# One fixed work list for another: the same 1368 tasks of a fused attention and MLP kernel, reordered

## The chip, the cores and the metric

The kernel runs on one core of a Trainium2 chip. The core's engines run their own instruction streams beside each other and meet only at semaphores: TensorE (PE, the matrix unit, with its weight loads shown as PEld), VectorE (DVE), ScalarE (ACT), GpSimd (POOL), and SyncE (SP), whose queue here issues nearly all DMA transfers. The metric is the device time of one execution in microseconds (us); the time given for a kernel is the median of its runs.

## The reference

A pre-norm block on 2048 tokens of width 640, in bfloat16, with two halves:

```
h  = x + attention(layernorm(x)) @ wo        # 32 heads of 20, four segments of 512 tokens
h2 = h + silu(layernorm(h) @ w1) @ w2        # 640 -> 1728 -> 640
```

Inside a segment the attention is causal softmax. From the second segment on, each head also reads a memory: with `phi(t) = t + 1 if t > 0 else exp(t)`, a matrix `M` and a vector `z` collect `phi(k)^T v` and the sum of `phi(k)` of all earlier segments, `a_mem = phi(q) M / (phi(q) z + 1e-6)`, and the output is `g * a_mem + (1 - g) * a_dot` with `g = sigmoid(beta)` of the head.

## The kernel before

The kernel is a graph of 1368 small tasks. Each is declared once (lines 550 to 1215) with the buffers that it reads and writes, its possible engines, and a function that emits its instructions. A list that is written out in the kernel, the string `ORDER`, fixes three things: the order of all tasks (each engine runs its own tasks in the order in which they stand in the list), the engine where a task has a choice (`/A` ACT, `/D` DVE, `/S` SP), and the buffer slots that a task opens (the numbers after the colon: PSUM banks, and slots of small rotating buffers). A tracker derives the semaphore waits from the reads and writes. There is no planner at run time: the list is the schedule.

The token dimension is cut into 16 blocks of 128 (`b`) and four segments of four blocks (`s`). The names in the list are these, in the order in which one segment's data passes through them:

- Loads: `x0` to `x12`, `w_wv`, `w_q`, `w_k`, `beta`, `w_wo`, `w_w1_0` to `w_w1_4`, `w_w2_0` to `w_w2_5` (lines 562 to 574). `beta` is a broadcast of 64 bytes to each of 128 partitions. `fillN` is N matmuls on zeros that have no use but to keep TensorE active (L599). `re_wq*`, `re_wk*` copy the raw weights into head groups (L677 on ACT, L679 on DVE); the raw weights land in the tile `sT`.
- Layer norm: `n1_st` (statistics, DVE, L706 and L709), `n1_rs` (POOL, L715 and L717), `n1_ap` (DVE, L723). For the first four blocks the transposition is done on TensorE, `n1_tp` (L732), and copied out by `n1_te` (ACT L741 or DVE L742); for all others by a DMA, `n1_tr` (L747).
- Projections: `v` (L774) and its evacuation `ve` (ACT L784, DVE L785); `pr` + segment + group + 0 for q or 1 for k (L808), its evacuation `qe` (ACT L816, DVE L817); `ex` (exponential, ACT L823) and `ph` (DVE L830, L833) make phi; `vt` are DMAs that build the head groups 5 to 7 (L844).
- Scores: `qk` (L880) computes a score set of four heads into four PSUM banks. The number after its colon is the first bank, so `:0` is banks 0 to 3 and `:4` is banks 4 to 7; two ACT exponentials `e...0` and `e...2` (L891) read two banks each into `PTA`, `PTB` or `PTE`; `mk` masks the diagonal on POOL (L903); `av` multiplies with v (L926). A tick is then finished by `oe` (ACT L939, DVE L941), `tn` (TensorE, L955 and L959), `nm` (DVE, L972 to L992) and `ad` (POOL, L1000). In segment 0 the score sets carry the suffixes `x`, `ya` and `yb` after the group; in the later ones `a`, `b`, `e` after `8 * s + g`.
- Memory of a segment: `kt` (DMA transposition), `mz` (L1048), `ma` (L1077), `mb` (POOL, L1084).
- Output projection and MLP: `ot` (DMA transposition), `wo` (L1109), `rs` (DVE, L1117), `n2_*` (the second layer norm, as above), `h1` (L1143, its narrow last slice L1138), `th` (tanh, ACT, L1152), `s` (DVE, L1158), `h2` in four parts (L1176), `o` (DVE, L1186), `out` (store).

Nearly all `qk` of a segment use the same four banks as the `qk` before them. Such a `qk` can start only when both exponentials of the set before have read those banks, and ACT can start on the new set only when the `qk` is done. Between the two sets ACT has work only if the list puts some other ACT task there.

Of the kernel before, what the change touches and what calls it, by code (L numbers as in the profile page):

```python
# [324 lines left out]
D = 640  # L325
# [45 lines left out]
n1_ap7:3 epsg1 oe4x/D:0 ve12/D kt02:0 n1_tr7 w_w1_2/S w_w2_0/S kt00:1 w_w1_3/S ex011:0 mk1yb mk5x mt0 qk6x0:4 av0y:2
e6x0:1 e6x2 tn4x:3 oe0y/D:0 av5x:0 tn3x:1 oe5x/A:1 qk7x0:4 e7x2:0 e7x0 nm4x:3 v10:2 nm3x:0 qk2ya0:4 ph041:2
n1_st10:2 ve10/D e2ya0:0 e2ya2 n1_rs11 mta2 mk7x n1_st9:3 n1_rs10 v13:0 mk6x tn0y:2 av7x:3 ve13/D nm0y:1 qk2yb0:4
oe7x/A:0 e2yb2:0 e2yb0 tn5x:3 tn7x:0 nm7x:2 av1y:1 av6x:2 qk3ya0:4 oe6x/D:1 nm5x:3 w_w1_4/S tn6x:2 nm6x:0 ot1:0
w_w2_5/S ot0 w_w2_4/S w_w2_1/S oe1y/A:0 e3ya0:1 e3ya2 ph011:1 pr101:1 mtb3 mz02:2 mk2yb av2y:3 qk3yb0:4 e3yb0:1
e3yb2 ma02/D:0 mz00:2 tn1y:0 oe2y/D:1 n1_ap11:1 qe101/D:0 pr100:3 qk4ya0:4 e4ya0:0 e4ya2 mk3yb ex031:2 nm1y:1
qe100/D wo1:0 av3y:3 qk4yb0:4 e4yb2:0 e4yb0 ma00/D:1 tn2y:2 ex101:1 rs1 wo0:0 oe3y/D:0 n2_st1:5 nm2y:2 kt04:0 tn3y:3
n2_rs1 nm3y:3 rs0 qk5ya0:4 pr140:2 n1_rs8 mk4yb pr121:3 e5ya0:1 e5ya2 qe140/A:0 qk5yb0:4 e5yb2:1 e5yb0 ex140:0
pr141:0 av4y:2 n2_ap1:0 n2_st0:4 n2_rs0 n2_ap0:2 kt01:1 n2_tr1:0 qk6ya0:4 qe141/D mk5yb pr120:1 ph031:0 oe4y/D:1
pr111:0 qe121/D:0 e6ya0:0 e6ya2 qk6yb0:4 qe120/D ex121:2 av5y:3 n2_tr0 h1_0_7_0:1 h1_0_0_0:2 e6yb2:0 e6yb0 qk7ya0:4  # L380
th0_7_0:0 ph101:2 qe111/D:0 oe5y/D:0 tn4y:0 s0_7_0:0 th0_0_0:1 h1_0_8_0:3 nm4y:0 s0_0_0 mz01:1 mz04:0 ma01/D:2
h1_0_3_0:2 e7ya2:1 e7ya0 th0_8_0:0 ma04/D:3 s0_8_0 th0_3_0:1 s0_3_0 tn5y:1 qk7yb0:4 e7yb2:1 mk6yb e7yb0 mk7yb mta0
av6y:0 mtb0 oe6y/A:1 h1_0_12_0:3 h1_0_1_0:2 qk8a0:4 th0_1_0:0 e8a2:0 e8a0 th0_12_0:1 s0_1_0 pr110:0 nm5y:1 qe110/D
h1_0_10_0:2 av7y:1 qk8e0:4 oe7y/D:0 th0_10_0:0 s0_12_0 pr130:0 s0_10_0 e8e2:0 e8e0 h1_0_5_0:2 h1_0_11_0:3 qk8b0:4
th0_5_0:1 n1_ap8:3 qe130/D:0 th0_11_0:0 w_w2_2/S kt03:1 tn7y:0 s0_5_0 nm7y:2 mz03:1 s0_11_0 h1_0_2_0:2 e8b2:0 e8b0
ma03/D:4 h1_0_6_0:0 th0_2_0:1 h1_0_13_0:1 th0_13_0:0 qk9a0:4 pr131:3 s0_2_0 s0_13_0 n1_ap10:0 h1_0_4_0:1 h1_0_9_0:2
qe131/D e9a2:1 e9a0 mk8a mk8e mm0 th0_6_0:1 th0_4_0:0 ex100:1 s0_6_0 mm4 mk8b mm6 qk9b0:4 vt19:0 th0_9_0:1 mm2 mm8
n1_rs9 mtb2 s0_4_0 w_w2_3/S vt16 vt10 vt18 e9b2:1 e9b0 av8:3 h2_0_0:0 h2_0_1 qk10a0:4 s0_9_0 ph100:0 ex141:1 ph121:1
e10a2:0 e10a0 h2_0_2 tn6y:2 h2_0_3 ph141:0 ex120:2 mk9a qk10b0:4 oe8/D:0 nm6y:3 o0 mzc0 mzc6 ph120:0 mzc2 h2_1_0:2
mk9b mm10 mzc4 e10b0:0 kt10:0 vt15 mm1 mzc1 mb00:0 e10b2 mk10a mzc5 mzc8 mm7 mzc7 mb03:0 mk10b ex111:1 n1_tr10:0  # L390
tn8:0 vt11 n1_tr8 nm8:0,0 h2_1_1 vt13 ot2 ot3 qk10e0:4 ph111:2 vt111 kt12:1 vt17 vt110 vt12 h2_1_2 av9:0 h2_1_3
ex110:2 ph110:0 oe9/D:1 e10e0:1 e10e2 qk11a0:4 mk10e mm3 mzc3 mb01:0 wo3:0 ad8:0 n1_ap9:2 o1 n1_tr9 vt14 e11a2:1
n1_tr11 e11a0 ex131:1 av10:2 mk11a mzc10 qk11b0:4 e11b0:1 e11b2 mk11b mb02:0 mm9 mzc9 rs3 oe10/D:0 tn9:0 wo2:2
qk12a0:4 nm9:1,1 v20:0 rs2 n2_st3:6 ex130:2 ph130:0 e12a2:0 e12a0 av11:2 qk13a0:4 n2_st2:7 mz12:3 ma12 ve20/A:0
# [851 lines left out]
```

## Time and profile before

| | us |
|---|---|
| median of 3 runs (305.32 to 306.07) | 305.46 |
| span of the profiled execution | 303.9 |
| TensorE busy / idle in the span | 290.1 / 13.8 |
| ScalarE (ACT) busy | 226.8 (75%) |
| VectorE (DVE) busy | 219.1 (72%) |
| GpSimd (POOL) busy | 143.9 (47%) |
| share of the chain that ended last: PE / ACT / DVE / DMA | 72% / 12% / 7% / 4% |

The span runs from the first to the last instruction of one profiled execution; the median of the runs lies 1.5 us above it. A busy time is the time in which an engine had an instruction running. For TensorE that is an upper bound of useful work, since the end of a matmul is modelled and a matmul in flight counts as busy while the next waits. TensorE's share is 95% over the whole span, but the other engines' shares are averages over stages with different limits: ACT has hardly anything to do in the last 55 us, which belong to the MLP of the last two segments, and is busy nearly all the time in some earlier stretches.

### The profile page before, as it was taken

The numbers are of one execution on the slowest core, as the hardware profiler recorded it, in microseconds if no ns is written. First come the engines' busy times: TensorE is split into PE (matmuls) and PEld (weight loads), VectorE is DVE, ScalarE is ACT, GpSimd is POOL, SyncE is SP. The second block draws the span as 40 slices with busy tenths as digits, with TensorE's granted clock in tenths as the row PEclk, the third lists the DMA queues.
The fourth block names the chain that finished last, engine by engine and source line by source line (L and its number), as shares of the span: only waits on it lengthen the run. The fifth ranks groups of instructions, "written<-read, shape, count | busy, mean of one in ns | idle before, by whom it ended". The sixth has DMA issues, their size and how long they took to land.

```text
span 303.9 us, 7238 instructions
## 1 busy us (share of the span) xinstructions
PE 290.1 (95%) x2876; PEld 165.8 (55%) x2900; DVE 219.1 (72%) x489; ACT 226.8 (75%) x322; POOL 143.9 (47%) x280
## 2 busy tenths in 40 slices
PE   8799889999999999999999999999999999999995
PEld 5434454466555455566644545566564466764573
DVE  5677997886788877877989886558767486835523
ACT  4599998999989889989789899968878941005310
POOL 4237673525677856535758328434873730300000
PEclk9999999999999999999999999999999999999999
DMA  6678487643153130056561500043250004332001
GB/s 194 216 211 240 79 202 179 130 106 90 38 110 61 41 41 2 4 102 64 132 170 22 67 17 19 2 77 62 36 108 2 0 2 88 80 88 72 0 24 65
DMA packets 48433, 24.64 MB, mean 81 GB/s; under 512 B 38864, under 2 KB 47312, under 8 KB 48400
## 3 DMA queue, kind: packets, MB, share of 16 engines
q1 hardware_dynamic: 47728, 23.09, 33.9%
q10 hardware_dynamic: 672, 1.10, 1.2%
q8 instruction: 23, 0.38, 0.5%
q14 instruction: 10, 0.08, 0.1%
HBM read 10.41 MB, written 2.62 MB: 43 GB/s over the span
## 4 chain that ended last, share of the span: by engine, by line
PE 72%; ACT 12%; DVE 7%; DMA 4%; issue 2%; POOL 1%; SPq 1%; DVEq 0%; ACTq 0%
PE ps_all L1176 18%; PE ps_all L1143 16%; PE ps_all L808 12%; PE ps_all L1109 7%; PE ps_all L880 6%; PE ps_all L926 5%; ACT PTA L891 4%; ACT PTB L891 3%; DMA sT<-in_A_wq_dram 3%; PE ps_all L774 2%; PE ps_all L955 2%; ACT PTE L891 2%; PE ps_all L959 1%; DMA oT<-otok 1%; PE ps_all L1048 1%
## 5 line engine op out<-in xcount | busy, mean ns | idle before, releaser
L891 ACT ACTIVATE PTA<-ps_all 128x1024 bf16<-128x1024 f32 x64 | 62.1, 1027 | 7.1 <-PE ps_all L880 6.5
L1176 PE MATMUL ps_all<-w_sb,sT 128*128 128x320 bf16 x448 | 65.2, 299 | 0.0
L891 ACT ACTIVATE PTB<-ps_all 128x1024 bf16<-128x1024 f32 (+1 forms) x64 | 58.9, 971 | 5.9 <-PE ps_all L880 5.6
L1143 PE MATMUL ps_all<-hT,w_sb 128*128 128x512 bf16 (+1 forms) x315 | 60.1, 335 | 0.9 <-issue 0.5
L1152 ACT ACTIVATE th<-ps_all 128x512 f32<-128x512 f32 (+2 forms) x70 | 34.0, 507 | 35.3 <-PE ps_all L1143 26.8
L1158 DVE SCALAR_TENSOR_TENSOR sT<-th,ps_all 128x512 bf16<-128x512 f32 (+2 forms) x70 | 38.0, 561 | 27.0 <-ACT th L1152 25.8
L903 POOL TENSOR_SCALAR_AFFINE_SELECT PTB<-PTB 128x512 bf16<-128x512 bf16 x64 | 41.3, 647 | 32.6 <-ACT PTB L891 30.3
L1176 PEld LDWEIGHTS ps_all<-w_sb,sT 128*128 128x128 bf16 x448 | 42.3, 98 | 19.3 <-issue 2.1
L1143 PEld LDWEIGHTS ps_all<-hT,w_sb 128*128 128x128 bf16 x325 | 30.3, 98 | 23.9 <-issue 1.3
L891 ACT ACTIVATE PTE<-ps_all 128x1024 bf16<-128x1024 f32 (+1 forms) x40 | 35.4, 943 | 2.2 <-PE ps_all L880 2.1
L903 POOL TENSOR_SCALAR_AFFINE_SELECT PTE<-PTE 128x512 bf16<-128x512 bf16 x40 | 26.0, 649 | 20.3 <-ACT PTE L891 18.8
L706 DVE BATCH_NORM_STATS2 stt<-x_tok 128x6 f32<-128x320 bf16 x64 | 27.9, 477 | 1.6 <-DMA x_tok<-in_A_x_dram 1.4
L808 PE MATMUL ps_all<-xT,wqr 128*128 128x512 bf16 x92 | 23.4, 380 | 1.9 <-ACT xT L741 1.1
L774 PE MATMUL ps_all<-wv_sb,xT 128*128 128x320 bf16 x160 | 24.3, 300 | 0.7 <-DMA xT<-xn_rot 0.4
L1109 PE MATMUL ps_all<-wo_sb,oT 128*128 128x320 bf16 x160 | 24.1, 299 | 0.8 <-DMA oT<-otok 0.5
L1000 POOL TENSOR_TENSOR otok<-on 128x320 bf16<-128x320 bf16 x24 | 19.0, 793 | 11.3 <-DVE on L992 11.3
L808 PE MATMUL ps_all<-xT,wkr 128*128 128x512 bf16 x94 | 23.4, 380 | 0.5 <-issue 0.3
L903 POOL TENSOR_SCALAR_AFFINE_SELECT PTA<-PTA 128x512 bf16<-128x512 bf16 x24 | 15.5, 647 | 16.5 <-ACT PTA L891 16.4
L1186 DVE SCALAR_TENSOR_TENSOR x_tok<-ps_all,x_tok 128x640 bf16<-128x640 f32 x16 | 13.0, 818 | 13.8 <-PE ps_all L1176 13.8
L880 PE MATMUL ps_all<-QK 20*128 20x256 bf16 (+3 forms) x360 | 20.5, 286 | 1.7 <-ACT PTB L891 0.7
L992 DVE TENSOR_TENSOR on<-ps_all,rd 128x640 bf16<-128x640 f32 x24 | 19.8, 825 | 0.8
L715 POOL TENSOR_TENSOR rst<-mvt,eps_c 128x1 f32<-128x1 f32 x32 | 7.0, 219 | 27.9 <-DVE mvt L709 24.9
(79 smaller groups left out, 412.6 us busy)
## 6 DMA issues: line engine op xcount, KB each, us to landing
out_dram<-x_tok SPq DMA_DIRECT2D x16, 160.0 KB, 1.9
w_sb<-in_B_w_dram SPq DMA_DIRECT2D x4, 432.0 KB, 6.0
w_sb<-in_B_w_dram SPq DMA_DIRECT2D x3, 480.0 KB, 4.3
x_tok<-in_A_x_dram SPq DMA_DIRECT2D x2, 640.0 KB, 4.4
QKV<-QK SPq DMA_DIRECT2D x16, 72.0 KB
wv_sb<-in_A_wv_dram SPq DMA_DIRECT2D x1, 800.0 KB, 5.6
sT<-in_A_wq_dram SPq DMA_DIRECT2D x1, 800.0 KB, 7.8
sT<-in_A_wk_dram SPq DMA_DIRECT2D x1, 800.0 KB, 9.6
```

The lines of the kernel that those rows point to most:

```text
L706: T.add(DV, lambda e, hh=hh: e.bn_stats(out=stt[:, s, 6 * hh:6 * hh + 6], in_=xb[:, 320 * hh:320 * hh + 320]), reads=R((xa, xsub)), writes ...
L774: fns.append(lambda e, c=c, hh=hh: e.matmul(bank(ps, hh)[:, 0:320], lhsT=xT[:, c, 128 * i:128 * i + 128], rhs=wv_sb[:, c, 320 * hh:320 * h ...
L808: fns = [lambda e, kc=kc: e.matmul(bank(ps)[:, lo:hi], lhsT=wt[:, kc, c, :], rhs=xT[:, kc, lo:hi], start=(kc == 0), stop=(kc == NC - 1)) f ...
L880: fns.append(lambda e, j=j, o=o, r=r, q0=q0, q1=q1, qa=qa, ka=ka: e.matmul(ps_all[:, o:o + q1 - q0], lhsT=ka[32 * r:32 * r + DH, 128 * j:1 ...
L891: T.add(AC, lambda e: e.activation(out=pt[:, pta.slot, q0:q0 + 2, 0:width], in_=sc3[:, b0:b0 + 2, 0:width], func=ACT.Exp, scale=SCALE), re ...
L903: fns.append(lambda e, v=v: e.affine_select(out=v, in_=v, pattern=[[0, 4], [1, 128]], compare_op=ALU.is_ge, fill=0.0, base=0, channel_mult ...
L992: T.add(DV, lambda e: e.tensor_tensor(out=on[:, ona.slot, :, :].rearrange("p b (x e) -> p b x e", e=DH), in0=v[:, :, :, 0:DH], in1=r2.unsq ...
L1109: fns.append(lambda e, c=c, hh=hh: e.matmul(bank(ps, hh)[:, 0:320], lhsT=oT[:, c, 128 * i:128 * i + 128], rhs=wo_sb[:, c, 320 * hh:320 * h ...
L1143: fns = [lambda e, c=c: e.matmul(bank(ps)[:, lo:hi], lhsT=w1_sb[:, c, 128 * f:128 * f + 128], rhs=hT[:, c, lo:hi], start=(c == 0), stop=(c ...
L1152: T.add(AC, lambda e: e.activation(out=th[:, tha.slot, lo:hi], in_=bank(ps)[:, lo:hi], func=ACT.Tanh, scale=0.5), reads=R((ps, [0])), writ ...
L1158: T.add(DV, lambda e: e.scalar_tensor_tensor(out=sT[:, f, lo:hi], in0=th[:, tha.slot, lo:hi], scalar=1.0, in1=bank(ps)[:, lo:hi], op0=ALU. ...
L1176: fns.append(lambda e, f=f, t0=t0, fr=fr, hh=hh: e.matmul(bank(ps, hh)[:, 0:320], lhsT=sT[:, f, t0:t0 + 128], rhs=w2_sb[:, fr, 320 * hh:32 ...
```

## The change

The string `ORDER` is replaced by another one, of the same 1368 tasks. It was annealed in a replay of the trace: order on each engine, engine of the evacuations, and slots. No task's function is touched, and every matmul, exponential and transfer is still there. What differs, beyond many swaps of neighbours:

- Start. `x1, x0, x2, x3` are loaded ahead of `w_wv`, `w_q`, `w_k`, and `beta` comes after `w_k` (before: `x0, x1, w_wv, x2, x3, beta, w_q, w_k`). The 31 `fill` matmuls of the start stand in one row (before: 21, then 6 and 4 between later transpositions). `v01` comes after all transpositions, and the `pr`/`qe` and `re_*` tasks of the first groups change order and engine.
- Queues. `x8` and `w_w1_0` move from ACT's DMA queue to SP's; the order of the MLP weights on SP is another one.
- Engines. 45 tasks change engine. In the projections of the last segment `qe310, qe311, qe321, qe340, qe341, ve31, ve33` go from ACT to DVE; `oe22, oe24` from DVE to ACT. In the middle of the list `ve23, qe211, qe230` go from DVE to ACT, `qe221, oe14` from ACT to DVE.
- TensorE's order is the same from the second score set on but for swaps over short distances, until the end of the last segment's attention. There `wo12, wo13, wo15, wo14` (before `wo14, wo12, wo15, wo13`) and the `h1_3` and `h2` groups of the last two segments take another order.

```diff
-zpad:0 x0:0 x1:1 w_wv:0 x2:2 x3:3 beta w_q:0 w_k halfc warm:0 iota vpad0 sel n1_st0:0 n1_st1:1 epsc mt3 vpad1 n1_rs0
-n1_rs1 epsg0 n1_ap0:0 fill21:0 n1_tp0:0 n1_te0/A:0 n1_ap1:1 fill6:2 n1_tp1:2 n1_te1/A v00:0 v01:2 n1_st2:2 n1_rs2
-n1_st3:3 n1_rs3 mt1 mt2 mta1 n1_ap2:2 n1_ap3:3 n1_tp2:4 n1_te2/D re_wq1/A:0 fill4:6 n1_tp3:6 n1_te3/A pr010:6
-re_wk1/D:0 re_wk0/D re_wk3/D x4/S:4,5,6,7 pr011:4 re_wk2/D re_wq4/D qe011/D:0 ve00/A:0 re_wk4/A qe010/A re_wq2/A
-lsc0 pr001:0 ve01/D lsc1 lsc2 re_wq0/A qe001/A:0 qk1x0:4 e1x2:0 pr000:1 qe000/D lsc3 pr021:0 e1x0 mk1x qk0x0:4
...
-kt20:0 ve32/D e22b2:1 e22b0 pr330:1 ex241:2 th1_8_0:0 qk23a0:4 e23a0:0 e23a2 pr310:2 qe310/A:0 qe330/D:0 pr301:3
-ex310:0 s1_8_0 tn19:0 qk22e0:4 ph221:2 qe301/D:0 pr300:2 pr311:3 e22e0:1 e22e2 qk23b0:4 ex240:1 qe311/A ph241:1
...
-th2_5_0:0 s2_5_0 th2_10_0:0 s2_12_0 h2_8_0:2 h2_11_0:4 h1_2_11_0:7 h2_8_1 h2_11_1 ad30 ot14:0 th2_11_0:1 wo14:0
-s2_10_0 s2_11_0 ot12 rs14 n2_st14:2 ot15 wo12:6 rs12 n2_st12:3 wo15:0 h2_11_2 h2_11_3 h2_8_2 rs15 n2_rs14 ot13
...
+iota:0 zpad warm:0 sel halfc x1:8 fill4:6 fill21:0 fill6:2 n1_st1:2 vpad1 mt3 x0:5 x2:0 n1_st0:0 x3:1 n1_st2:1 w_wv:0
+epsc mt0 n1_rs1 n1_rs0 n1_ap0:0 n1_ap1:1 n1_rs2 n1_st3:3 n1_tp0:0 n1_tp1:4 mt1 n1_rs3 vpad0 n1_ap2:2 n1_ap3:3 n1_te0/A:0
+v00:6 n1_te1/A w_q:0 w_k n1_tp3:0 n1_tp2:2 v01:4 n1_te3/A re_wq0/D:0 re_wq1/D ve01/D:1 re_wk1/D:0 re_wq3/D n1_te2/A
+pr000:1 pr010:0 qe010/D:0 ve00/A re_wq4/A re_wk0/A re_wk4/D beta re_wq2/A lsc0 pr011:2 pr001:3 re_wk2/D qe001/D:0
+re_wk3/A qe011/A qk1x0:4 e1x2:1 e1x0 ex001:0 pr020:2 qe020/A:0 pr021:0 qe000/D qk0x0:4 e0x2:0 pr041:3 e0x0 x4/S:2,4,3,11
...
+e22b2 s1_0_0 pr330:3 s1_8_0 qk23a0:4 ve32/D e23a2:1 tn19:0 qe330/D:0 pr301:2 pr310:3 e23a0 qk22e0:4 nm19:3,0 ex201:0
+ph201:1 qe310/D:0 pr311:0 mk22b ad21 ex221:2 e22e2:1 pr300:3 e22e0 qk23b0:4 ex241:0 ph240:0 e23b2:0 e23b0 qe311/D kt20:1
...
+h1_2_10_0:1 ad28 mk31b mk31a th2_3_0:0 tn29:6 tn30:4 av31:3 oe31/A:1 h1_2_5_0:0 s2_3_0 nm30:0,0 ad30 tn31:2 th2_5_0:0
+th2_10_0:1 nm29:1,1 nm31:3,0 s2_5_0 h2_10_0:4 h2_9_0:6 h1_2_11_0:2 th2_11_0:0 s2_11_0 s2_10_0 h2_10_1 h1_2_12_0:3
+h2_10_2 ad29 th2_12_0:1 s2_12_0 ad31 ot12:0 wo12:0 rs12 n2_st12:7 ot13 wo13:2 rs13 ot15 h2_9_1 wo15:0 n2_st13:3 n2_rs13
```

## The prediction

> **What bounds the kernel now.** The page first: engine shares, then the chain that ended last.
>
> ```profile
> span 303.9 us, 7238 instructions
> PE 290.1 (95%) x2876; PEld 165.8 (55%) x2900; DVE 219.1 (72%) x489; ACT 226.8 (75%) x322; POOL 143.9 (47%) x280
> ...
> PE 72%; ACT 12%; DVE 7%; DMA 4%; issue 2%; POOL 1%; SPq 1%; DVEq 0%; ACTq 0%
> ```
>
> TensorE looks like the bound and its matmuls stay the same, so the 13.8 us in which it idles would be all there is to win. But a busy TensorE is not a TensorE at its peak, and 12% of the chain is ACT. So the second view is the table of stages (columns: length, busy PE, PEld, DVE, ACT, POOL with instructions, clock, DMA share, GB/s).
>
> ```profile
> 25.00:42.00 17.00, 15.15 (x195) 8.06 (x193) 14.26 (x39) 16.33 (x24) 11.65 (x26) 1.00 0.54 122
> 42.00:100.00 58.00, 55.94 (x672) 32.62 (x677) 46.91 (x117) 54.61 (x79) 34.22 (x76) 1.00 0.49 112
> 100.00:116.00 16.00, 15.32 (x167) 7.73 (x167) 13.24 (x27) 13.52 (x17) 9.62 (x17) 1.00 0.27 38
> 116.00:142.00 26.00, 25.15 (x285) 15.57 (x287) 19.37 (x43) 24.82 (x39) 13.66 (x23) 1.00 0.27 44
> 142.00:160.00 18.00, 17.26 (x189) 9.82 (x190) 16.20 (x32) 14.61 (x20) 11.89 (x20) 1.00 0.65 137
> 160.00:196.00 36.00, 35.37 (x323) 17.77 (x327) 27.69 (x59) 34.65 (x50) 18.91 (x34) 1.00 0.18 27
> 196.00:243.00 47.00, 46.42 (x484) 26.01 (x486) 31.19 (x64) 39.08 (x49) 28.21 (x47) 1.00 0.25 46
> ```
>
> ACT is as full as PE in three stretches: 94 to 96% from 25 to 100 us, 95% from 116 to 142, 96% from 160 to 196. There a microsecond off ACT's path can be a microsecond off the end. Elsewhere ACT has room and PE sets the pace. The third view, the timeline, shows what opens the ACT stretch.
>
> ```profile
> 11.58 0.83 ACT L677 ACTIVATE wqr<-sT 128x400 bf16<-128x400 bf16 x2 [3.46 <-DMA sT<-in_A_wq_dram]
> ...
> 13.28 1.03 PE L808 MATMUL ps_all<-xT,wqr 128*128 128x512 bf16 x4 [1.13 <-ACT xT L741]
> ```
>
> ACT waits 3.46 us for the q weights; the first projection waits for the last transposed block, held behind that copy in ACT's order. The fourth, ACT's timeline, shows what ACT still idles on later: a score set on the same banks, with no ACT task in between.
>
> ```profile
> 30.91 1.51 ACT L891 ACTIVATE PTE<-ps_all 128x768 bf16<-128x768 f32 x2 [0.45 <-PE ps_all L880]
> 49.45 1.51 ACT L891 ACTIVATE PTB<-ps_all 128x768 bf16<-128x768 f32 x2 [0.45 <-PE ps_all L880]
> ...
> 204.79 1.94 ACT L891 ACTIVATE PTA<-ps_all 128x1024 bf16<-128x1024 f32 x2 [0.94 <-PE ps_all L880]
> ```
>
> **The change part by part, against the profiled 303.9 us** (the median of the runs is 1.5 us more; I add the same).
>
> *Start.* x1 issues at 0.81 and lands after 2.27 us as x0 did, so statistics of x1, x0, x2 run from 3.1 to 6.2 (1.04 each). `ap0` needs POOL's second pair (0.83 and 0.99): 6.4 to 6.85, `ap1` to 7.2, `st3` to 8.2, `ap2`, `rs3` (0.99), `ap3` to 9.95. On PE the fills run at 213 ns until the clock rises near 5.9, then at 109: 31 of them end at 6.8. Then transposition of block 0, its copy to 8.1, `v00` 8.25 to 9.7, blocks 3 and 2 to 10.8, their copies (0.70) on ACT to 11.8, `v01` to 12.25, and the first `pr` at 12.3 against 13.28. Two `pr` with q (1.09 each), then k: DVE has done `ve01` by 13.1 and `re_wk1` by 13.4, so k only has to land by 13. Four `pr` end at 16.6 and the first scores start at 16.7 against 16.52, with one `pr` more done. Carried through ACT's order to the end of set 2's exponentials: 24.0 against 23.86, but 14.57 us of ACT work done instead of 13.33 (`ex021`, `ex011` are in). ACT's idle sum there is 9.4 instead of 10.5: **-1.1**. Ends: 0 if weights land no earlier than now and the slack is eaten, -1.7 if also the 0.6 us before set 2 goes.
>
> *Order of the loads.* The table of stages again, for the windows before, in and after beta's packets, says why the weights should come earlier:
>
> ```profile
> 4.00:6.50 2.50, 2.50 (x19) 1.72 (x17) 1.65 (x6) 0.24 (x1) 1.74 (x5) 1.00 1.02 345
> 6.50:9.00 2.50, 2.34 (x21) 1.50 (x19) 1.53 (x5) 1.17 (x2) 0.00 (x0) 1.00 0.55 170
> 9.00:11.50 2.50, 2.26 (x20) 1.36 (x17) 1.68 (x5) 0.00 (x0) 2.12 (x7) 1.00 1.04 378
> ```
>
> The last column falls to 170 GB/s where the 128 packets of beta pass: 2.5 x (1 - 170/378) = 1.4 us lost. With beta last, q lands near 10.2 and k near 12.4 instead of 11.56 and 13.76. The chain above needs q at 12 and k at 13, so this is already in the -1.1. [...]
>
> *Clock.* With all fills in front, PE has small gaps between 6.8 and 12.3 (longest 0.4 us). Before, it has one of 1.13 us at 12.15 and the granted clock stays 1.00; so 0. [...]
>
> *Score sets without cover.* Going through ACT's list, 17 sets on the same banks have no ACT task ahead of them before, 14 after. The 17 idle 10.7 us in all in the timeline, 0.63 each. By place: one more between 24 and 60 us (+0.2, since two neighbours had 0.1 each), the one at 91 us gone (-0.9), two at 106 to 111 gone. I count only those before 100 us: **-0.7** (ends +0.4 and -1.9, all of them).
>
> *Evacuations moved.* 116 to 142 us: `qe211`, `qe230` come to ACT (0.6 each), `oe14` leaves (0.69): **+0.5** (0 to +1.2, with `ve23`). 160 to 196: seven leave ACT (5 x 0.6, 2 x 0.7 = 4.4), two come (2 x 0.69): -3.0 on ACT's work, which has 1.4 us of idle there. PE must follow, and it idles 0.6 us there beside what hides in its busy time. I take less than half, **-1.3** (0 to -3.0). DVE has 36 - 27.7 = 8.3 us free and takes 5 x 0.69 + 2 x 0.82 - 2 x 0.66 = 3.8. From 196 to 243 ACT has 8 us free: 0, ends -1.4 and +0.5.
>
> *Waits on PE.* 317 of PE's instructions wait instead of 308, 5 more for two semaphores. The nearest row is weight loads on "issue", 4.2 us in 16 times: 0.26. 9 x 0.26 = 2.4 as the upper end, 0 as the lower, most of them long satisfied: **+0.3**.
>
> *Queues on SP.* `x8`, `w_w1_0`: 0.64 us off ACT's queue, where it waited for scores anyway: 0. `w_w2_0` and `w_w2_1` now issue behind a `vt` that waits for `qe110` (done at 71.6): issue near 73 and 74.5; `w_w2_3` took 4.33 us to land, so 77.5 and 79.5, for use at 80.5 and 81.4. Hidden by 2 us. `ot7` goes behind `ot5` and a `vt`: lands near 134.9 for `wo7` at 134.7: 0.2, taken as 0. At the end four transpositions (1.3 each) stand in one row, the last issued 4.5 us after `wo14` and landing 2.65 later, at 7.1; the eight `h2` parts between last 7.6 (before: 6.6 of 7.6). Hidden by 0.5. The end itself, `h2` - `o` - `out`, stays.
>
> Sum: -1.1 - 0.7 + 0.5 - 1.3 + 0.3 = -2.3, span 301.6, median **303.2**.
>
> **The rivals.**
> - *PE is the wall.* PE is at 96 to 98% in every stretch after 42 us, so ACT's relief lies beside it and only the start pays, less the added waits: -1.1 + 0.3 = -0.8, 304.7. For it: 1.0 to 2.1 us of PE idle per stretch. Against: by the table of waits, the weight loads of the scores stood 6.8, 4.0 and 3.9 us behind the exponentials into PTB, PTA and PTE.
> - *ACT's path converts whole:* -1.1 - 1.9 + 0.5 - 3.0 + 0.3 = -5.2, 300.3. Against: PE would need to shed 5 of 13.8 us of idle, 3 of which are at the end.
> - *Slower: DVE's queue from 160 to 196.* The seven evacuations now stand on DVE behind `s` (0.56) or `rs`; if each is late by one such op and PE waits for its bank, that is 7 x 0.56 = 3.9 in place of the -1.3: -1.1 - 0.7 + 0.5 + 0.3 + 3.9 = +2.9, 308.4; half of them late, 306.4. It decides from 1.0 us in total to lose the gain, 1.9 to be slower. For it: DVE goes from 77 to 87% there. Against: those banks are opened a `qk` or more ahead.
>
> **How the numbers follow.** 0.3% is 0.9 us, about what a measurement can tell from no change. Likeliest case 0.48, whole conversion 0.15, wall 0.17, slower 0.20. Of the likeliest a tenth falls within 0.9 us, of the wall a third is faster: faster 0.63, same 0.17, slower 0.20. The likeliest's own range is 301.8 to 304.6; with the other cases, and the tail of the slower one cut, 300.2 to 306.9.
>
> **What would show it.** First `pr` at 12.3, set 2's exponentials done near 24 with `ex011` before them; the windows of beta's packets no longer ahead of q and k; ACT below 92% from 160 to 196 and that stretch shorter by a microsecond; 14 score sets with ACT idle before them. It is wrong if PE waits on DVE's `QK` or `Vx` copies there, if `wo7` or the first `h1_3` waits for a DMA, or if the granted clock drops in the first 13 us.

## The result and the profile after

The changed kernel takes 309.84 us (median of 4 runs, 308.27 to 313.05) against 305.76 us (305.32 to 306.17, 4 runs) of the kernel before on the same chip: a ratio of 1.0109, 95% interval 1.0075 to 1.0144, so 3.3 us slower (2.3 to 4.4). One of its four runs (313.05 us, granted clock 0.994) is a slow one, and the ratio leaves it out. The profiled execution spans 307.7 us (before: 303.9). The prediction said 303.2, range 300.2 to 306.9.

The page of the changed kernel: the span, the engines' busy time and the chain that ended last. (The changed list has three lines fewer, so a line of the kernel stands three lower here than before: L808 is L805. In the experiments it is two.)

```profile
span 307.7 us, 7240 instructions
PE 291.2 (95%) x2876; PEld 165.3 (54%) x2900; DVE 223.7 (73%) x491; ACT 225.6 (73%) x320; POOL 143.8 (47%) x280
...
PE 67%; DVE 11%; ACT 8%; DMA 8%; SPq 2%; issue 2%; POOL 1%; DVEq 0%; ACTq 0%
```

ACT lost 1.2 us of work, as intended, and its share of the chain fell from 12% to 8%. But DVE rose from 7% to 11%, DMA from 4% to 8% and SP's queue from 1% to 2%. The chain did not get shorter; it goes round ACT, over transfers and DVE. (24 of the 2900 matmul records are missing in this profile and in that of before, so TensorE's busy time is not compared below.)

The table of stages, with the columns of the one shown before:

```profile
42.00:100.00 58.00, 54.08 (x647) 30.62 (x650) 45.15 (x113) 52.92 (x78) 31.44 (x70) 1.00 0.58 118
100.00:116.00 16.00, 15.03 (x167) 7.79 (x166) 14.21 (x28) 13.99 (x18) 11.55 (x20) 1.00 0.22 43
116.00:142.00 26.00, 25.14 (x278) 15.46 (x277) 19.48 (x44) 24.84 (x39) 13.93 (x24) 1.00 0.36 63
142.00:160.00 18.00, 17.85 (x200) 10.36 (x200) 14.52 (x34) 14.32 (x19) 9.88 (x18) 1.00 0.31 65
160.00:196.00 36.00, 34.52 (x309) 16.23 (x313) 29.79 (x62) 32.30 (x44) 17.84 (x30) 1.00 0.20 44
196.00:243.00 47.00, 45.67 (x485) 26.17 (x486) 34.76 (x67) 38.40 (x49) 28.52 (x47) 1.00 0.27 46
```

From 160 to 196 us ACT's busy time falls from 34.65 to 32.30 and DVE's rises from 27.69 to 29.79, as the prediction asked; yet fewer matmuls and fewer weight loads fit into the same 36 us (309 against 323, 313 against 327). From 42 to 100 us 650 weight loads fit instead of 677: the largest loss is there. Eight evacuations changed engine in that stretch, five of them from DVE to ACT, and DVE has less to do there than before (45.15 us against 46.91).

To place the loss, the two executions are set beside each other by the work that TensorE has done: after equal work, how much later is the changed kernel? The table has the kernel before's own time in the first column and, in us, how far each kernel lies behind it (negative: ahead). It is worked out from the start times of TensorE's instructions in the four traces and stands in no view; where neighbours in the order were swapped, a single value can be off by some tenths. `e3_four` and `e12_four_vt` are experiments, told below.

| before at | after | e3_four | e12_four_vt |
|---|---|---|---|
| 18.3 | -1.33 | -0.10 | -1.41 |
| 56.1 | -1.07 | +0.16 | -1.16 |
| 60.9 | +0.41 | +0.16 | -1.16 |
| 92.1 | +1.28 | +0.16 | -1.16 |
| 125.4 | +1.90 | +0.25 | -1.08 |
| 151.3 | +2.21 | +0.94 | -0.25 |
| 161.4 | +1.48 | +0.21 | -0.99 |
| 166.2 | +2.30 | +2.00 | -0.15 |
| 175.3 | +2.85 | +2.38 | +0.06 |
| 224.5 | +2.51 | +2.05 | -0.27 |
| 228.7 | +3.78 | +2.29 | -0.03 |
| 302.3 | +3.71 | +2.52 | +0.20 |

The start is won (1.3 us, of which 1.1 are left at 56), and it is lost again in steps: +1.5 near 60 us, +0.5 near 92, +0.8 at 166 and 0.6 behind it, +1.3 at 231 of its own time. At each of the four places TensorE has a gap with DVE behind it. The first, in DVE's timeline of the changed kernel (columns: start, length, line, operation, out<-in, idle before and what ended it):

```profile
56.91 0.32 DVE L971 TENSOR_TENSOR otok<-ps_all,rd 128x160 bf16<-128x160 f32 x1
58.63 0.29 DVE L827 TENSOR_SCALAR phiK<-QK 128x512 bf16<-128x512 bf16 x1 [1.40 <-DMA phiKt<-phiK]
58.96 0.88 DVE L830 TENSOR_TENSOR phiK<-phiK,ex 128x512 bf16<-128x512 bf16 x1
59.77 0.75 DVE L720 TENSOR_SCALAR xn_rot<-x_tok,mvt,rst 128x640 bf16<-128x640 bf16 x1
60.44 0.87 DVE L703 BATCH_NORM_STATS2 stt<-x_tok 128x6 f32<-128x320 bf16 x2
61.34 0.21 DVE L706 BATCH_NORM_AGGREGATE mvt<-stt 128x2 f32<-128x12 f32 x1
61.47 0.64 DVE L814 CAST QK<-ps_all 128x512 bf16<-128x512 f32 x1
```

and in TensorE's:

```profile
59.24 1.25 PE L805 MATMUL ps_all<-xT,wkr 128*128 128x512 bf16 x4
62.16 0.60 PE L805 MATMUL ps_all<-xT,wqr 128*128 128x512 bf16 x2 [1.67 <-DVE QK L814]
```

`ph031` (L827) writes a slot of `phiK` from which the DMA transposition `kt01` still reads. `kt01` is issued at 53.82, behind two weight loads whose issue took 2.61 us, and lands at 58.61. DVE runs its tasks in the list's order, so it idles 1.40 us, and behind it stand `n2_ap0`, `n1_st10` and the evacuation `qe141` (the CAST at 61.47), for whose bank `pr120` waits: 1.67 us. In the kernel before, the same instruction came at 60.66, four tasks later in DVE's order and after `qe141`; `kt01` landed at 57.91, only 0.7 us earlier, and nothing waited for it:

```profile
60.05 0.68 DVE L817 CAST QK<-ps_all 128x512 bf16<-128x512 f32 x1
60.66 0.28 DVE L830 TENSOR_SCALAR phiK<-QK 128x512 bf16<-128x512 bf16 x1
```

The other steps have the same form, except the last. DVE and then TensorE of the changed kernel:

```profile
91.78 0.81 DVE L720 TENSOR_SCALAR xn_rot<-x_tok,mvt,rst 128x640 bf16<-128x640 bf16 x1 [0.96 <-DMA xT<-xn_rot]
...
163.23 0.89 DVE L703 BATCH_NORM_STATS2 stt<-x_tok 128x6 f32<-128x320 bf16 x2 [0.99 <-DMA x_tok<-in_A_x_dram]
...
227.00 0.75 DVE L827 TENSOR_SCALAR phiQ<-QK 128x512 bf16<-128x512 bf16 x1
...
229.19 0.80 DVE L830 TENSOR_TENSOR phiQ<-phiQ,ex 128x512 bf16<-128x512 bf16 x1
...
230.52 0.82 DVE L989 TENSOR_TENSOR on<-ps_all,rd 128x640 bf16<-128x640 f32 x1
```

```profile
94.04 0.40 PE L923 MATMUL ps_all<-PTA,Vx 128*32 128x512 bf16 x4 [0.68 <-DVE x_tok L1183]
...
165.96 1.25 PE L1140 MATMUL ps_all<-hT,w_sb 128*128 128x512 bf16 x5 [0.64 <-DVE sT L1155]
...
231.40 0.40 PE L923 MATMUL ps_all<-PTA,Vx 128*32 128x512 bf16 x4 [0.96 <-DVE on L989]
```

Near 92, `n1_ap9` waits for the landing of `n1_tr8`, which SP issues behind `ot3` and `ot2`. At 163, `n1_st12` waits for `x12`; `x12` may be loaded only when the four `out` stores of the first segment have landed, and SP issues the last two behind `vt24`, `vt29`, `vt210` (x12 lands at 163.21; before 160.09). At 231, no transfer is involved: `nm27`, which ends with the last of these DVE lines, stands behind `ph340` and `ph320` (from 227.00 to 229.99), and `av28` waits for it.

### The profile page after: what moved, and what is told of

Same layout as the page of the kernel before. It is cut to its first block, busy times and chain, and to the rows that moved or that the text cites. A ratio compares the mean times of both kernels' runs of the same rounds, so it can differ in the third digit from the quotient of the medians.

```text
span 307.7 us, 7240 instructions
## 1 busy us (share of the span) xinstructions
PE 291.2 (95%) x2876; PEld 165.3 (54%) x2900; DVE 223.7 (73%) x491; ACT 225.6 (73%) x320; POOL 143.8 (47%) x280
## 4 chain that ended last, share of the span: by engine, by line
PE 67%; DVE 11%; ACT 8%; DMA 8%; SPq 2%; issue 2%; POOL 1%; DVEq 0%; ACTq 0%
PE ps_all L1173 18%; PE ps_all L1140 15%; PE ps_all L805 10%; PE ps_all L877 6%; PE ps_all L1106 5%; PE ps_all L923 5%; ACT PTE L888 3%; PE ps_all L771 3%; ACT PTA L888 2%; DMA x_tok<-in_A_x_dram 2%; DVE stt L703 2%; DMA xT<-xn_rot 2%; PE ps_all L952 2%; DMA phiKt<-phiK 2%; PE ps_all L1045 1%
## 5 line engine op out<-in xcount | busy, mean ns | idle before, releaser
L1140 PE MATMUL ps_all<-hT,w_sb 128*128 128x512 bf16 (+1 forms) x315 | 60.8, 336 | 1.7 <-DVE sT L1155 0.6
L1155 DVE SCALAR_TENSOR_TENSOR sT<-th,ps_all 128x512 bf16<-128x512 f32 (+2 forms) x70 | 37.3, 558 | 22.4 <-ACT th L1149 22.2
L900 POOL TENSOR_SCALAR_AFFINE_SELECT PTE<-PTE 128x512 bf16<-128x512 bf16 x40 | 25.9, 647 | 18.5 <-ACT PTE L888 17.1
L805 PE MATMUL ps_all<-xT,wqr 128*128 128x512 bf16 x94 | 23.7, 380 | 2.5 <-DVE QK L814 1.7
L805 PE MATMUL ps_all<-xT,wkr 128*128 128x512 bf16 x92 | 23.2, 380 | 0.8 <-issue 0.7
L814 DVE CAST QK<-ps_all 128x512 bf16<-128x512 f32 x28 | 18.7, 679 | 6.1 <-PE ps_all L805 5.9
```

Source lines behind the costliest of these rows:

```text
L805: fns = [lambda e, kc=kc: e.matmul(bank(ps)[:, lo:hi], lhsT=wt[:, kc, c, :], rhs=xT[:, kc, lo:hi], start=(kc == 0), stop=(kc == NC - 1)) f ...
L900: fns.append(lambda e, v=v: e.affine_select(out=v, in_=v, pattern=[[0, 4], [1, 128]], compare_op=ALU.is_ge, fill=0.0, base=0, channel_mult ...
L1140: fns = [lambda e, c=c: e.matmul(bank(ps)[:, lo:hi], lhsT=w1_sb[:, c, 128 * f:128 * f + 128], rhs=hT[:, c, lo:hi], start=(c == 0), stop=(c ...
L1155: T.add(DV, lambda e: e.scalar_tensor_tensor(out=sT[:, f, lo:hi], in0=th[:, tha.slot, lo:hi], scalar=1.0, in1=bank(ps)[:, lo:hi], op0=ALU. ...
```

## The experiments

Two theories. *A*: the loss is made where a transfer lands late while a DVE task that needs it stands at the head of DVE's queue. *B*: DVE is simply given too much (it is busy 4.6 us longer). Every kernel below runs the same 1368 tasks. The ratios are to 17 to 21 runs of the kernel before on the same chip (median 306.8 us for the first four kernels, 306.4 for the others); beside them stands the changed kernel's 1.0109.

**e1_phi_back: one task of the changed list put back.**

```diff
-pr141:2 ph031:0 n2_ap0:3 n1_st10:3 qe141/D
+pr141:2 n2_ap0:3 n1_st10:3 qe141/D ... pr120:2 ph031:0
```

> The changed kernel with one task of DVE's order put back: ph031 behind qe141, where the kernel before has it, instead of ahead of n2_ap0, n1_st10 and qe141. Theory A (a DVE instruction at the head of its queue waits for a late transfer, and all behind it is late): in the changed kernel ph031 waits until 58.61 us for the transposition kt01, DVE idles 1.40 us, qe141 ends at 62.11 and pr120 waits 1.67 us; with the task behind qe141 that wait is gone and the kernel is 1.5 to 1.8 us shorter than the changed one (about 308.0 against 309.8 in the median, span near 306). Theory B (DVE simply has too much to do after the moved evacuations from 160 to 196 us): no more than 0.3 us, since the wait turns up at the next place.

308.92 us, ratio 1.0073 (1.0044 to 1.0102): 1.1 us less than the changed kernel's, by intervals that overlap. The gap at 60 us is gone from the trace; the one at 166 us, where `x12` is late, has grown from 0.64 to 1.65 us. A and B can't be told apart by this time alone.

**e2_w1_early: `kt01` made earlier by putting the two weight loads ahead of it.**

```diff
-w_w1_0/S ot1:0 ot0 ... w_w1_4/S w_w1_2/S kt01:1
+w_w1_0/S w_w1_4/S w_w1_2/S ot1:0 ot0 ... kt01:1
```

> The changed kernel with DVE's order untouched; only on SP's queue the loads w_w1_4 and w_w1_2 go ahead of ot1, into a stretch from 44.9 to 47.1 us in which SP has nothing to issue, so that kt01 is issued straight after kt04. Theory A: kt01 lands near 54 instead of 58.6, ph031 does not wait, and the gain is the same 1.5 to 1.8 us as from moving ph031, so the cause is the transfer and not the place in DVE's order alone. Theory B, or that the wait of ph031 is for something else: no gain, within 0.3 us.

312.86 us, 1.0167 (1.0103 to 1.0231): no gain, and by the medians 3.0 us slower than the changed kernel, though the intervals overlap; neither theory expected that. `kt01` lands at 55.33, as wanted, but now `ot1` is the one behind the weights and lands at 53.64 (49.66 in the changed kernel, 50.86 in the kernel before). TensorE's timeline, and windows before, in and after what follows (the last three columns are clock, DMA share, GB/s):

```profile
53.69 2.33 PE L1107 MATMUL ps_all<-wo_sb,oT 128*128 128x320 bf16 x10 [2.49 <-DMA oT<-otok]
```

```profile
51.00:54.30 3.30, 0.81 (x13) 0.46 (x6) 1.05 (x4) 2.38 (x4) 1.09 (x2) 0.99 1.28 125
54.30:57.70 3.40, 3.40 (x35) 1.57 (x34) 1.61 (x3) 0.76 (x2) 0.00 (x0) 0.50 0.11 23
57.70:61.00 3.30, 3.30 (x28) 1.85 (x27) 2.62 (x8) 3.19 (x5) 2.22 (x5) 1.00 0.00 0
```

A stall of 2.49 us, and then the granted clock is 0.50 for 3.4 us. Three of the four runs had a mean clock of 0.994 or 0.995 and took 312.33 to 313.55 us; the fourth had 0.999 and took 309.61, level with the changed kernel. Here who waits is only exchanged: `kt01` lands 3.3 us earlier than in the changed kernel, `ot1` 4.0 us later.

**e3_four: four of the gaps mended by order alone.** `ph031` behind `qe120`; `n1_tr8` ahead of `ot3`; `n1_st15` behind `s1_12_0`; `ph340` and `ph320` behind `nm27` and `nm28`.

```diff
-pr141:2 ph031:0 n2_ap0:3
+qe120/D ph031:0 qe111/A:0
-ot3 ex110:1 qk10b0:4 ot2 n1_tr8:0
+n1_tr8:0 ot3 ex110:1 qk10b0:4 ot2
-n1_st15:2 n1_rs12 th1_2_0:0 mk20a n1_rs15
+s1_2_0 s1_12_0 n1_st15:2 n1_rs15
-tn27:6 ph340:0 h2_7_1 h2_7_2 ph320:0 nm27:1,1
+tn27:6 h2_7_1 h2_7_2 nm27:1,1 ph340:0 ... nm28:3,0 ph320:0
```

> The changed kernel with four repairs at the four places where it falls behind the kernel before by over half a microsecond: ph031 behind qe120; the transposition n1_tr8 issued ahead of ot3 and ot2 (n1_ap9 waits 0.96 us for it); n1_st15 and its n1_rs15 behind s1_12_0 (both wait for the late load x12); ph340 behind nm27 and ph320 behind nm28. Theory A: the four cost 1.7, 0.75, 0.6 and 1.2 us, together 4.2, so the time comes to about 305.5, 4 us below the changed kernel and level with the kernel before. Theory B: under 1.5 us gained, the lag moves on to other places.

308.03 us (10 runs), 1.0046 (1.0017 to 1.0075): 1.9 us less than the changed kernel, which lies between A's 4.2 and B's 1.5. The table above shows more than the time does: the steps at 60 and 92 us are gone whole, that at 231 is 0.24 instead of 1.27. Together that is 3.0 us. Two other things took part of it back: the v weights landed at 9.70 instead of 8.25 (the start's lead is 0.1 instead of 1.3), and the step at 166, where `x12` is still late, is 1.8 instead of 0.8. No engine was changed, so DVE's load is the same, and B cannot explain the 3.0.

**e12_four_vt: the same, and the three `vt` out of the stores' way.**

```diff
-vt22 n2_tr5:0 ... n2_tr4 vt24 vt29 vt210 out3 out2 mz14:1 x12/S
+vt22 vt24 vt29 vt210 n2_tr5:0 ... n2_tr4 out3 out2 mz14:1 x12/S
```

> The kernel of e3_four with vt24, vt29 and vt210 issued behind vt22, near 138 us, instead of between n2_tr4 and the stores out3 and out2 near 152 us. Set beside each other by the work that TensorE has done, e3_four lies level with the kernel before up to 162 us and 2.0 us behind it at 168 us, where n1_st12 on DVE waits for x12, and x12 for the stores, which took 4.1 us to land beside these transfers (2.1 us in the kernel before). Theory: x12 then lands near 160 instead of 163.0, the time falls by 1.4 to 1.8 us, ratio 0.999 to 1.000. If the stores are slow for another reason, x12 lands after 162 and the gain is below 0.5 us.

306.56 us (11 runs), 1.0009 (0.9975 to 1.0043): level with the kernel before. Against e3_four that is 1.1 us by the ratios, less than expected, and the intervals overlap; what the move did is read from the trace. `x12` lands at 160.36. SP's timeline in e3_four, then in this kernel:

```profile
151.92 2.10 SPq L842 DMA_DIRECT2D QKV<-QK  x3
154.07 1.99 SPq L1188 DMA_DIRECT2D out_dram<-x_tok  x2
158.67 0.40 SPq L560 DMA_DIRECT2D x_tok<-in_A_x_dram  x1
```

```profile
151.94 0.82 SPq L1188 DMA_DIRECT2D out_dram<-x_tok  x2
155.99 0.40 SPq L560 DMA_DIRECT2D x_tok<-in_A_x_dram  x1
```

The two stores issue in 0.82 instead of 1.99 us and 2.1 us earlier; they still take 3.6 us from the last issue to the last landing (4.1 in e3_four, 2.1 in the kernel before), so that part of the expectation, that the three transfers slow them, holds for half a microsecond only. By the table the step at 166 us falls from 1.8 to 0.8. The profiled execution also had its v weights early (7.97), which is worth 1.3 us of its span but belongs to no move.

So five repairs, nine tasks moved and no engine changed, take the changed list from 1.0109 (1.0075 to 1.0144) to 1.0009 (0.9975 to 1.0043). A carries four of the five: `kt01`, `n1_tr8`, and `x12` twice. The fifth, `nm27`, is a matter of order on DVE without any transfer. B, a load on DVE that order could not mend, is not needed.

**e6_before_evac: the evacuations alone, in the old order.**

```diff
-qe310/A:0 ... qe311/A ... qe321/A ... qe340/A ... qe341/A:0 ... ve31/A ... ve33/A ... oe22/D:0 ... oe24/D:1
+qe310/D:0 ... qe311/D ... qe321/D ... qe340/D ... qe341/D:0 ... ve31/D ... ve33/D ... oe22/A:0 ... oe24/A:1
```

> The kernel before with nine engines changed and no order: qe310, qe311, qe321, qe340, qe341, ve31, ve33 on DVE, oe22, oe24 on ACT. The prediction's step on the evacuations between 160 and 196 us: -1.3 us (0 to -3.0). Its rival of the wall: 0 (within 0.4). Its slower rival, DVE's queue at this place: +3.9, or about half of it. If the new list's loss has nothing to do with the load on DVE, the wall or the step must hold; if DVE's load alone loses time here, it shows as +0.6 or more.

313.14 us, 1.0211 (1.0182 to 1.0239): 6.5 us slower, more than the price of my slower rival. TensorE, then DVE:

```profile
182.81 0.40 PE L878 MATMUL ps_all<-QKV 20*128 20x384 bf16 x8
186.02 1.29 PE L772 MATMUL ps_all<-wv_sb,xT 128*128 128x320 bf16 x6 [2.82 <-DVE on L990]
```

```profile
182.91 0.69 DVE L815 CAST QK<-ps_all 128x512 bf16<-128x512 f32 x1 [1.69 <-PE ps_all L806]
183.52 0.64 DVE L828 TENSOR_SCALAR phiK<-QK 128x512 bf16<-128x512 bf16 x1
184.19 0.43 DVE L831 TENSOR_TENSOR phiK<-phiK,ex 128x512 bf16<-128x512 bf16 x1
184.53 0.18 DVE L984 TENSOR_TENSOR rd<-ps_all,epsg 128x32 f32<-128x32 f32 x1
184.75 0.35 DVE L989 RECIPROCAL rd<-rd 128x32 f32<-128x32 f32 x1
185.14 0.82 DVE L990 TENSOR_TENSOR on<-ps_all,rd 128x640 bf16<-128x640 f32 x1
```

DVE is not full here: it idles 1.69 us, waiting for a projection, and after that everything due stands in one row. `v33` waits for the bank that `nm19`, the last in the row, frees. TensorE is idle for 2.82 us there, 1.37 and 0.90 elsewhere, 5.1 in three gaps, and after the longest the granted clock is 0.57 from 186.1 to 189.5 us and 0.93 from 189.5 to 193.0.

**e9_after_nine_back and e10_four_nine_back: the same nine engines put back in the new list and in e3_four.**

```diff
-qe310/D:0 qe311/D qe321/D qe340/D qe341/D ve31/D ve33/D oe22/A oe24/A:1
+qe310/A:0 qe311/A qe321/A qe340/A qe341/A ve31/A ve33/A oe22/D oe24/D:1
```

> The changed kernel with the nine evacuations of the last segment back on the engines that they had before (qe310, qe311, qe321, qe340, qe341, ve31, ve33 on ACT, oe22, oe24 on DVE), the new order kept. In the order of before these moves alone cost 2.1%. Theory: they load DVE at the place where its queue already stands behind late transfers, in the new order too; then the time falls by 1 us or more, to a ratio of 1.007 or less (the changed kernel: 1.011). Rival: the new order was fitted to them; then ACT is late instead, and the ratio stays at 1.009 to 1.015.

> The kernel of e3_four, whose DVE no longer waits for kt01 and n1_tr8, with the same nine evacuations back. If they still cost something there, ratio 1.002 or less (e3_four: 1.0046); if the new order needs them, 1.005 to 1.010.

322.6 us, 1.0513 (1.0467 to 1.0559), and 321.95, 1.0497 (1.0462 to 1.0531). Both theories of the first missed by far; of the second, "the new order needs them" had the sign. In e9 TensorE:

```profile
186.65 1.80 PE L772 MATMUL ps_all<-wv_sb,xT 128*128 128x320 bf16 x7 [2.53 <-ACT QK L814]
```

It is the mirror image of e6: `v33` now waits 2.53 us for `qe311` on ACT, which has to finish the two exponentials that stand ahead of it (1.94 us). Gaps of 1.44, 1.24 and 2.65 us follow by 212 us, the granted clock is 0.95 from 160 to 196 us and 0.89 from 196 to 243. An evacuation has no price of its own here: the same nine moves cost 6.5 us in one order, and their reverse 12.4 us (1.0513 against 1.0109) in the other.

**The start: e4_before_head, e7_head_wv, e5_before_beta, e11_head_tp_ot6.** e4 is the kernel before with the new list up to the third score set `qk2x0`; e7 the same with the v weights loaded third, as before; e5 the kernel before with only `beta` moved; e11 is e4 with `n1_tp2` in TensorE's wait for the v weights and `ot6` earlier.

```diff
 e4:  -zpad:0 x0:0 x1:1 w_wv:0 ... qk2x0:4
      +iota:0 zpad warm:0 sel halfc x1:1 fill4:6 fill21:0 ... qk2x0:4
 e7:  -x0:0 x2:2 n1_st0:0 x3:3 n1_st2:2 w_wv:0
      +x0:0 w_wv:0 x2:2 n1_st0:0 x3:3 n1_st2:2
 e5:  -x3:3 beta w_q:0 w_k
      +x3:3 w_q:0 w_k beta
 e11: -n1_te0/A:0 v00:6 n1_te1/A ... vt211:0 ot6:0
      +n1_te0/A:0 n1_te1/A n1_tp2:2 v00:6 n1_te2/A ... ot6:0 vt211:0
```

> The kernel before with the first part of the new list alone, up to the third score set (qk2x0); from there the old list. The prediction's first step, alone: 1.1 us shorter than the kernel before (0 to 1.7), so about 304.6 in the median; in the trace the score set qk2x0 starts 1.1 us earlier. If the lead at the start is eaten by ACT's saturated stretch that follows, 0.

> The kernel before with the new list's start, as in e4_before_head, but the v weights are loaded third, ahead of x2 and x3, as before. Theory: in the new start the first projection waits for the v weights, which land 0.9 to 2.3 us later than before behind x2 and x3; then they land near 7.4 here, the gap ahead of v00 (0.84 to 2.34 us in the runs with the new start) closes to below 0.4, and the time is another 0.3 to 0.9 us shorter than that of e4_before_head (ratio to the kernel before about 0.995). Rival: x2 and x3 are then late by as much and the gap goes to the transpositions of blocks 2 and 3; the ratio stays at 0.997.

> The kernel before with one task moved: beta is issued behind the k weights. The prediction's step on the loads says that beta's 128 packets cost the weights 1.4 us: the q weights then land 1.0 to 1.4 us earlier than in the kernel before (near 10.3), the k weights near 12.5, and the time falls by 0.7 to 1.1 us, since ACT's wait of 3.46 us in front of the first copy of the q weights shrinks by as much. Rival: the order of the tasks made the start shorter and not the loads; then the weights land earlier and the time falls by 0.3 us at most, because the transpositions and their copies stand in ACT's way all the same.

> The kernel of e4_before_head (0.9968 of the kernel before) with two more moves. First, n1_tp2 and its copy n1_te2 go ahead of v00 and of n1_te3, into TensorE's wait for the v weights (1.40 us in that run): the copies of blocks 2 and 3 end 0.7 us earlier, and the first pr starts at 11.8 instead of 12.39. Second, ot6 is issued ahead of vt211, 0.65 us earlier, and the gap of 0.54 us ahead of wo6 closes. Together 0.5 to 1.1 us: ratio 0.993 to 0.995. If the first projections only wait for the q weights instead, 0.3 us and 0.996.

e4: 305.49 us, 0.9968 (0.9950 to 0.9986), by the ratios faster than the two kernels by 1.0 and 4.3 us; of all versions run it has the lowest ratio, which e11 cannot be told apart from. e7: 309.17, 1.0088 (1.0057 to 1.0118), a clear miss. e5: 306.7, 1.0002 (0.9975 to 1.0029). e11: 305.53, 0.9974 (0.9955 to 0.9992): the gap ahead of `wo6` closed, but nothing is measurably added to e4.

e7 is the first theory once more, by accident. DVE's timeline:

```profile
4.24 0.83 DVE L704 BATCH_NORM_STATS2 stt<-x_tok 128x6 f32<-128x320 bf16 x2
5.10 0.21 DVE L707 BATCH_NORM_AGGREGATE mvt<-stt 128x2 f32<-128x12 f32 x1
8.05 0.89 DVE L704 BATCH_NORM_STATS2 stt<-x_tok 128x6 f32<-128x320 bf16 x2 [2.75 <-DMA x_tok<-in_A_x_dram]
8.98 0.21 DVE L707 BATCH_NORM_AGGREGATE mvt<-stt 128x2 f32<-128x12 f32 x1
9.10 0.75 DVE L721 TENSOR_SCALAR xn_rot<-x_tok,mvt,rst 128x640 bf16<-128x640 bf16 x2
```

`x2` lands at 8.03 behind the v weights. The new list has the statistics of `x2` ahead of `n1_ap0`, whose own inputs were there at 6.2. So the first transposition starts at 9.55 instead of 7.1, and after 3.49 us without work the granted clock of TensorE is 0.89 from 9 to 25 us.

e5 had its q weights at 9.75 instead of 11.56, 1.8 us earlier, and the first projection at 12.44 instead of 13.28. (Part of that is the execution: e6, which loads in the old order too, had them at 10.81.) Its profiled execution stays 0.98 us ahead of that of the kernel before until 129 us and ends 0.73 ahead, but the median of 12 runs (304.77 to 308.74) shows nothing, and the interval only just excludes a gain of more than 0.25%, 0.8 us. What `beta`'s place is worth is left open.

**e8_repair: e3_four with three more moves**: the v weights third, `out3` and `out2` ahead of the three `vt`, `n1_st12` behind `s1_12_0`.

```diff
-x2:0 n1_st0:0 x3:1 n1_st2:1 w_wv:0 ... n2_tr4 vt24 vt29 vt210 out3 out2 ... n1_st12:7 th1_12_0:1 ... s1_12_0
+w_wv:0 x2:0 n1_st0:0 x3:1 n1_st2:1 ... n2_tr4 out3 out2 vt24 vt29 vt210 ... th1_12_0:1 ... s1_12_0 n1_st12:7
```

> The four moves of e3_four, and three more: the v weights are loaded third; out3 and out2 are issued ahead of vt24, vt29 and vt210, so that x12, which waits for those stores, is issued earlier; n1_st12 and n1_rs12 stand behind s1_2_0 and s1_12_0 on DVE. If the new list loses only by transfers that land late in front of DVE's queue, x12 lands near 161.5 instead of 163.0, the gaps ahead of v00 (2.34 us) and h1_1_11_0 (0.72 us) close, and the time is 1.0 to 2.0 us shorter than that of e3_four: ratio to the kernel before 0.998 to 1.001. If the rest is spread DVE work (4.6 us more of it busy), the gaps close but less than 0.5 us comes back, ratio 1.003 or more.

312.61 us, 1.0206 (1.0166 to 1.0246). Every move only shifted the wait. The first fell into e7's trap (3.60 us). The third made `ma23` late (1.52 us). The second made the `vt` late:

```profile
160.89 0.62 PE L878 MATMUL ps_all<-QKV 20*128 20x384 bf16 x8 [2.25 <-DMA QKV<-QK]
```

The three `vt` had stood near 138 us in the kernel before; in the changed kernel SP issues nothing from 140.0 to 148.0 us, and it is there that e12 has room for them.

## Why the prediction was wrong

*The step that failed* is "Queues on SP". It picked some of the moved transfers, asked whether each lands before TensorE needs it, and priced all of SP's order at 0. For those that it named this held: `w_w2_0` landed at 79.5 and `w_w2_1` at 81.1 without a gap (predicted 77.5 and 79.5), `wo7` is no later than the kernel as a whole, and behind 250 us the lag stays at 3.7. But a transfer also holds up whoever *writes* what it reads, here by 1.40 us. `kt01`'s next writer, `ph031`, was moved four tasks up on DVE, which runs its tasks in the list's order; `n1_ap9` waits in the same way for `n1_tr8`, and `x12`, which writes what the stores read, comes late to DVE. None of the three was looked at. These three places cost 1.5, 0.5 and 0.8 us. A fourth step, 1.3 us, is no queue's: the sum had no term for DVE's tasks in another order, and `nm27` was put behind two tasks that it need not follow. Together that is 4.1 of the 4.8 us by which the lag grows between 56 and 302 us. Experiments e3 and e12 show it: with these places mended and all engines as in the changed list, the time is that of before.

The signs that the prediction named looked elsewhere. Of its signs of being wrong, none shows: no gap of TensorE from 160 to 196 us is for a `QK` or `Vx` copy on DVE (the one such wait is at 62), no matmul of `wo7` or the first `h1_3` waits for a DMA, and the profiled clock holds. Of its signs of being right, the start and ACT's share (90% from 160 to 196) came; the shorter stretch and the 14 score sets did not.

*The start, -1.1*, was right: `qk2x0` at 20.80 against 21.89 is 1.09, and alone it measured -1.0 (e4). On the way, the first `pr` began with its weight load at 11.79 (predicted 12.3; its first recorded matmul is at 12.10), set 2's exponentials ended at 23.29 (24.0), q and k landed at 10.50 and 12.70 (10.2 and 12.4). Not seen: the v weights, third in the old queue and fifth in the new, now decide `v00` in eight of the nine profiled executions that load them fifth. They landed between 7.97 and 9.95 there, with gaps of 0.5 to 2.3 us ahead of `v00`; in the earliest, e12, the wait was for a copy on ACT.

*The order of the loads*: in this pair of executions the q and k weights come 1.1 us earlier (1.8 in e5), but the nine executions with the changed order of loads had q anywhere from 10.42 to 12.16, the two with the old order at 10.81 and 11.56. So neither the 1.4 us lost to `beta`'s packets nor the lead is shown, and whether it is worth anything stays open; the sum held -1.1 once for loads and order, so it cost the prediction nothing.

*The clock, 0*: right for the profiled execution of the changed kernel; its longest gap, 1.67 us, left the clock at 1.00. But the run of 313.05 us had a mean clock of 0.994 over a span of 311.3. In e2, where the clock was 0.50 for 3.4 us, the mean over 311.8 us was 0.995, so about one such stretch would make that run's mean (an estimate; where it fell was not recorded). In e8 a gap of 2.25 us was followed by a clock of 0.51 from 161.0 to 164.4 us.

*Score sets without cover, -0.7*: wrong. ACT's idle time in front of the exponentials, released by a score set, went from 14.3 us (25 times) to 18.5 us (28 times). Fewer sets lack an ACT task ahead of them in the list, but when TensorE itself is late, ACT's cover is used up and it waits all the same. In e12_four_vt it is 14.8 us (25 times): the repairs take the loss away, and the 0.7 still does not appear.

*Evacuations moved, -1.3 (0 to -3.0)*: no gain is seen. ACT has 2.4 us less to do from 160 to 196, DVE 2.1 more, and e12 goes from -0.99 to 0.0 there, 0.8 of it where `x12` is waited for and the rest without a gain either. The end that I left out was the true danger: alone they cost +6.5. What I counted was free time on DVE (8.3 us); what mattered was where in DVE's order each evacuation stood. The +0.5 between 116 and 142 came out as about 0.1.

*Waits on PE, +0.3*: not to be told apart in any run.

*The rivals.* The slower one had the right engine and form, a task held up in DVE's queue, but the place (160 to 196 us) and the releaser (other evacuations) fit only the old order, where e6 is that rival and costs 6.5 instead of 3.9. The wall described what is left: repaired, the new list is level with the old one. (By the table of stages PE was at 96 to 99% after 42 us and idle for 0.6 to 2.1 us per stretch, not 1.0 to 2.1, which spoke more for the wall than the prediction allowed.) Why the won start then vanishes is only partly shown: of the 1.2 us that e12 still leads by at 92 us, 0.5 go near 131 us, where `wo6` waits 0.70 us for `ot6`; the others are steps of 0.2 to 0.3.

## What to carry to other kernels

When a list of tasks is reordered, follow each transfer both ways: to the reader that needs it, and to the next writer of the buffer that it reads, and ask what stands behind that writer in its engine's order. Busy shares do not show this: in e6 DVE, busy for 26.4 of the 36 us from 160 to 196, held up TensorE for 2.82 us by the order of its tasks. Engine choices and order are one choice: nine engine moves alone cost 6.5 us, undoing them in the new list cost 12.4, and the new start alone gained 1.0.

## What the runs showed of the hardware that was not expected

- **Half clock after short stalls.** In the profiled executions of e2, e6, e7, e8, e9 and e10 the mean granted clock was 0.979 to 0.995, in the other seven that recorded it 0.998 to 1.000. After a stall of TensorE of 2.49 us in e2 it was 0.50 from 54.3 to 57.7 us; after 2.82 us in e6, 0.57 from 186.1 to 189.5; after 2.25 us in e8, 0.51 from 161.0 to 164.4; after 2.53 us in e9, 0.52 from 187.0 to 190.5, and with the gaps of 1.44, 1.24 and 2.65 us there, 0.80 from 209 to 212 and 0.50 from 212 to 215. With the 3.49 us at the start of e7 and the 3.60 us at that of e8 it was 0.89 from 9 to 25 us. It was 1.00 after 1.13 us in the kernel before (12.0 to 17.0 us), after 1.40 us in e4 (9 to 25) and after 1.67 us in the changed kernel (61 to 64). The clock of e3_four, with 2.34 us ahead of `v00`, was not recorded. How long a stall it takes is not shown. By e2, 3.4 us at 0.50 cost up to 1.7 us on top of the stall (an estimate).
- **A DVE instruction beside GpSimd.** The TENSOR_SCALAR of `ph` (128x512, bfloat16) occurs 30 times in each trace. In the changed kernel's trace the 11 that had POOL idle all the while took 0.28 to 0.29 us, the 17 with POOL busy for over half took 0.56 in the mean, 0.87 at most, though three of them took 0.28 too; in the kernel before 10 took 0.28 and 16 took 0.49 in the mean. In all the 30 take 13.16 us in the changed kernel and 11.84 before, 1.3 of DVE's 4.6 us more; whether their place beside POOL is the cause was not tested.
- **Landing times wander.** The v weights, issued at 2.67 or 2.68 us in the same place of the queue, landed between 7.97 and 9.95 us in nine profiled executions. In these nine, a start that waits for them is uncertain by 1.0 us either way (half of the 1.98 us between the first and the last).
